# One bank per tile of h, two tiles to a PSUM pair, in an attention and feed-forward kernel

## The chip, the cores and the metric

The kernel runs on one core of one Trainium2 chip. The metric is the device time of one execution in microseconds (us). Matrix products run on TensorE (PE), elementwise work on VectorE (DVE), ScalarE (ACT) and GpSimd (POOL); SyncE (SP) issues DMAs. TensorE writes its results to PSUM, which ACT and DVE read. Each engine works its own list of instructions in order and waits on semaphores that the others raise.

## The reference

For each of 8 batches and 8 heads (576 tokens, head width 64) 32 pack vectors p attend to k and v, the tokens q attend to the packed result, and the outcome goes through a feed-forward layer with g(h) = h cos(h):

```
def sm_attn(qq, kk, vv):
    s = scale * np.matmul(qq, kk.transpose(0, 1, 3, 2))
    s = s - np.max(s, axis=-1, keepdims=True)
    a = np.exp(s)
    a = a / (np.sum(a, axis=-1, keepdims=True) + 1e-09)
    return np.matmul(a, vv)
p_packed = sm_attn(p, k, v)
out = sm_attn(q, p_packed, p_packed)
...
x = out.transpose(0, 2, 1, 3).reshape(4608, 512)
h = x @ w_in            # 512 x 2048
g = h * np.cos(h)
return g @ w_out        # 2048 x 512
```

## The kernel before, in words

**Stages.** A batch b passes through two stretches. In the first the scores are made, exponentials taken, sums and their inverses formed (functions `s1`, `s2`, `sums2`, `normalise`), and the packed values are multiplied into w_in, so that `PPW[b]` (written by `ppw`, four pieces of 512 columns) holds the weights of h for this batch, and `a2n[b]` the normalised second attention. In the second, the **slot** of the batch, h of its 576 tokens is made in 16 tiles of 128 rows, tile number `fc` from 0 to 15. Between tiles stand the output matmuls of the batch before.

**A tile of h before** (`h_mm`): it takes a PSUM pair from `psa()` (two banks of 512 fp32 columns; three pairs in turn in these stretches), splits the 576 tokens into two halves of 288, one to a bank, and makes four matmuls of 288 columns. ACT takes the cosine of both halves in one instruction (`cosT`, as a sine with a bias), and DVE multiplies both with it into `gT[b][:, fc, :]` in one instruction. After tiles 7 and 15 POOL copies tokens 512 to 575 of eight tiles to `joint`, which gathers the last 64 tokens of two batches for one output chunk of 128 tokens.

**Batch 0** is made otherwise: `h_one` makes a tile with tokens 0 to 511 alone, in a single bank, with two matmuls of 512 columns, a cosine and a multiply of 512 columns. Its last 64 tokens of all 16 tiles are made later in one go by `h_rest(0)`, called in slot 1: 32 matmuls of 64 columns into one pair, one cosine and one multiply of 1024 columns, straight into `joint`.

**Output shares.** `out_gen(b)` gives out the output matmuls of batch b one by one, 16 to a chunk of 128 tokens (512 columns each, L351). `fill(n)` puts n of them, called shares here, into TensorE's list. After 16 shares a chunk is copied out of PSUM (`osb`) by ACT in the slots and by DVE between them, and SP sends it to memory. `keep` shares are held back for after the slot.

**The order in a slot** is written out by hand (`slot`): tile fc, its multiply, then its quota of shares, with hooks behind certain tiles. `heavy` gives a tile a greater weight in the quota, and says how many of its shares come behind the hook; `{7: (5, 4)}` is such an entry. The hook after tile 7 (`tiled`) is called the burst here: two pieces of `ppw` for the slot's own batch, then `pp` of the next batch, which writes its result into the unused end of tile 7's pair (`spare`). At the last tile `pp_T` is put ahead of the multiply.

**PSUM and waits.** A pair is given out again when its readers are done. The recording layer works out from the tiles that each instruction reads and writes which others it must wait for, and puts semaphore waits into the lists. Since each engine works in order, whatever stands behind a waiting matmul in TensorE's list waits too.

Of the kernel before, what the change touches and what calls it, by code (L numbers as in the profile page):

```python
# [9 lines left out]
BF16 = mybir.dt.bfloat16  # L10
AF = mybir.ActivationFunctionType
ALU = mybir.AluOpType
PI_HALF = 1.5707963267948966

@with_exitstack
def kernel(
# [10 lines left out]
    nc = tc.nc  # L27
    B, H, S, D = q.shape
# [3 lines left out]
    NFC = DF // 128  # L32
    C = 6
    TP = S // C
    HS = S // 2
# [9 lines left out]
    g_pool = ctx.enter_context(tc.tile_pool(name="g", bufs=2))  # L45
    j_pool = ctx.enter_context(tc.tile_pool(name="joint", bufs=2))
    cos_pool = ctx.enter_context(tc.tile_pool(name="cos", bufs=3))
# [15 lines left out]
    V, ACT, G = nc.vector, nc.scalar, nc.gpsimd  # L63
# [17 lines left out]
    a2u, lns, a2n, PPW = {}, {}, {}, {}  # L81

    def copy(eng, out, in_):
        if eng is ACT:
            ACT.copy(out=out, in_=in_)  # L85
        else:
            eng.tensor_copy(out=out, in_=in_)  # L87

    def psa(dt=FP32):
        return psum["A"].tile([128, 2, 512 if dt == FP32 else 1024], dt, name="psA", tag="A")  # L90
# [5 lines left out]
    def behind(t):  # L96

        G.tensor_copy(out=gate, in_=t)  # L98
# [8 lines left out]
    def pe_T(n, b, engs=(V, V, V), groups=(0, 1, 2), own=None):  # L107
        if 0 in groups:
            xT[n, b] = att_pool.tile([128, H * 3, TP], BF16, name=n + "T", tag=n + "T", bufs=2 if n == "k" else 1)
        t = xT[n, b]  # L110
        flat = bf[n, b].rearrange("p h x -> p (h x)")
        for i in groups:
            ps = own(BF16) if own else psa(BF16)[:, 0, :]
            for j in range(8):
                o = 8 * i + j
                nc.tensor.transpose(ps[:, j * TP:(j + 1) * TP], flat[:, o * 128:(o + 1) * 128],  # L116
                                    ident[0:TP, 0:TP])
            to = t[:, 8 * i:8 * i + 8].rearrange("p a x -> p (a x)"), ps[:, 0:8 * TP]
            if engs[i] is None:
                return to  # L120
            copy(engs[i], *to)
# [72 lines left out]
    def pp_T(b, eng=V, own=None):  # L194
        ps = own(BF16) if own else psa(BF16)[:, 0, :]
        t = pp_sb[b % 2].rearrange("p a d -> p (a d)")
        for i in range(2):
            nc.tensor.transpose(ps[:, i * 128:(i + 1) * 128], t[:, i * D:i * D + 128], ident)
        copy(eng, ppT[b % 2].rearrange("p i x n -> p (i x n)"), ps[:, 0:256])
# [51 lines left out]

    gT, joint = {}, {}

    spare = [None]

    def h_mm(b, fc):
        if fc == 0:
            g_tile(b)
        ps = psa()
        spare[0] = ps[:, 1, HS:512]  # L260
        for y in range(2):
            for e in range(2):
                nc.tensor.matmul(ps[:, e, 0:HS], PPW[b][:, y, fc * 128:(fc + 1) * 128],  # L263
                                 a2n[b][:, y, e * HS:(e + 1) * HS], start=(y == 0), stop=(y == 1))
        cs = cos_pool.tile([128, S], BF16, name="cosT")
        csv = cs.rearrange("p (e x) -> p e x", e=2)
        ACT.activation(out=csv, in_=ps[:, :, 0:HS], func=AF.Sin, bias=PI_HALF)  # L267

        def rest():
            V.tensor_tensor(out=gT[b][:, fc, :].rearrange("p (e x) -> p e x", e=2),  # L270
                            in0=ps[:, :, 0:HS], in1=csv, op=ALU.mult)
            if fc % 8 == 7:
                j0 = (b % 2) * 64
                G.tensor_copy(out=joint[b // 2][:, fc - 7:fc + 1, j0:j0 + 64],  # L274
                              in_=gT[b][:, fc - 7:fc + 1, 512:576])
        return rest

    def g_tile(b):
        gT[b] = g_pool.tile([128, NFC, S], BF16, name="gT", tag="gT")
        if b % 2 == 0:  # L280
            joint[b // 2] = j_pool.tile([128, NFC, 128], BF16, name="joint", tag="joint")

    def h_one(b, fc, own=None):

        if fc == 0:
            g_tile(b)
        ps = (own or one)()
        for y in range(2):
            nc.tensor.matmul(ps, PPW[b][:, y, fc * 128:(fc + 1) * 128], a2n[b][:, y, 0:512],  # L289
                             start=(y == 0), stop=(y == 1))  # L290

        def cos():
            cs = cos_pool.tile([128, 512], BF16, name="cosT")
            ACT.activation(out=cs, in_=ps, func=AF.Sin, bias=PI_HALF)  # L294
            return lambda: V.tensor_tensor(out=gT[b][:, fc, 0:512], in0=ps, in1=cs, op=ALU.mult)  # L295
        return cos

    def h_rest(b):

        t = psa()  # L300
        for fc in range(NFC):
            for y in range(2):
                nc.tensor.matmul(t[:, fc // 8, (fc % 8) * 64:(fc % 8) * 64 + 64],  # L303
                                 PPW[b][:, y, fc * 128:(fc + 1) * 128], a2n[b][:, y, 512:576],
                                 start=(y == 0), stop=(y == 1))
        cs = cos_pool.tile([128, 2, 512], BF16, name="cosR", bufs=1)
        ACT.activation(out=cs, in_=t, func=AF.Sin, bias=PI_HALF)
        j0 = (b % 2) * 64
        V.tensor_tensor(out=joint[b // 2][:, :, j0:j0 + 64],
                        in0=t.rearrange("p a (f x) -> p (a f) x", x=64),  # L310
                        in1=cs.rearrange("p a (f x) -> p (a f) x", x=64), op=ALU.mult)
# [53 lines left out]
    def to_do():  # L365
        return sum(n for _, n in filler)

    def fill(n):
        while n > 0 and filler:
            next(filler[0][0])  # L370
            filler[0][1] -= 1
            if filler[0][1] == 0:
                filler.pop(0)
            n -= 1
# [109 lines left out]
    rest_ppw()  # L484
    fill(7)

    def slot(s, hooks, keep=0, heavy={}, last=None):


        left = to_do() - keep  # L490
        weight = [1 + heavy.get(fc, (0, 0))[0] for fc in range(NFC)]
        for fc in range(NFC):
            rest = h_mm(s, fc)
            if fc == NFC - 1 and last:
                last()
            rest()
            quota = (left * sum(weight[:fc + 1])) // sum(weight) - (left + keep - to_do())
            behind = min(quota, heavy[fc][1]) if fc in heavy else quota
            fill(quota - behind)
            while hooks and hooks[0][0] == fc:  # L500
                hooks.pop(0)[1]()
            fill(behind)

    def pw2(b, n, eng=None):
        ppw(b, n, eng)
        ppw(b, n + 1, eng)

    def tiled(b):


        own, later = spare[0], []
        for n in (2, 3):
            later += ppw(b, n, (ACT, V)[n - 2], later=True)
        later[0]()
        pp(b + 1, V, own=lambda: own)
        later[1]()
# [10 lines left out]
    def cross(n, b):  # L527
        return lambda: xbar(n, b)

    osb_eng[0] = ACT  # L530
    slot(1, [(2, lambda: pw2(1, 2, (ACT, V))), (4, lambda: h_rest(0)), (6, lambda: pack_p(2, 4)), (7, cross("k", 3)),
             (8, tk2), (9, cross("q", 2)), (10, lambda: pe_T("k", 2, (V, V, ACT), (2,)))], 4, {2: (1, 2), 4: (3, 5)})
    ACT.preload_act_table_set(EXP_SET)
    osb_eng[0] = V
    behind(xT["q", 2][0:1, 0, 0:1])
# [33 lines left out]
                                in_=p_bf[:, 8:2 * B].rearrange("p g t d -> p (g t d)"))  # L569
# [2 lines left out]
        load(n, b)  # L572
    fill(9)
    osb_eng[0] = ACT
    slot(2, [(7, lambda: tiled(2))], 10, {7: (5, 4)}, lambda: pp_T(3, V))

    for s in range(3, B):
        nxt = s + 1 < B
        ACT.preload_act_table_set(EXP_SET)
        osb_eng[0] = V  # L580
        set_filler(s - 1)
        fill(5)
        s2(s)
        ppw(s, 0, V)
        fill(8 if nxt else 9)
        if nxt:
            s1(s + 1)
            ppw(s, 1, V)
            a1_xbar(s + 1)
            xbar("q", s + 1)  # L590
            recips(s + 1)
            if s + 2 < B:
                xbar("k", s + 2)
                behind(xT["k", s + 2][0:1, 0, 0:1])
        else:
            for n in range(1, 4):
                ppw(s, n, V)
        fill(4 if nxt else 5)
        sums2(s, 0)
        fill(5)  # L600
        sums2(s, 1)
        normalise(s)
        ACT.preload_act_table_set(SIN_SET)
        fill(13)
        osb_eng[0] = ACT
        for n, b in (("v", s + 2), ("q", s + 2), ("k", s + 3)):
            if b < B:
                load(n, b)
        if nxt:
            slot(s, [(7, lambda: tiled(s))], 5 if s % 2 else 13, {7: (5, 4)}, lambda: pp_T(s + 1, V))  # L610
        else:
            slot(s, [], 5)
    set_filler(B - 1)
    fill(1000)
    tail_chunk(B - 1, 4)
# [30 lines left out]
```

## Time and profile before

| | |
|---|---|
| three runs, us | 245.00, 245.49, 246.91 |
| median | 245.49 |
| the profiled execution's own time | 245.1 |
| its span, first to last instruction | 243.3 |
| mean granted TensorE clock | 0.997 |
| ACT copies of output chunks, mean of one | 583 ns (128x512) |
| POOL copies to `joint` | 14, 8.6 us |
| DMA moved | 37.37 MB, mean 154 GB/s |

How to read the profile's lines. A group line names the kernel's line, engine and operation, what is written and read with partitions x elements, the count, then busy us in all, mean ns of one, and the idle time of the engine just ahead of them with what ended most of it. PEld is TensorE's weight load, which overlaps its matmuls. The chain is followed back from the last instruction: at each step to what released it, or to the instruction before it on its engine. A matmul's end in the profile is modelled and runs past the start of the next one, so its pitch is read from a run of several in the chain, and the idle time of TensorE is counted from that end. PEclk is the granted clock.

### The profile page before, as it was taken

How to read it: one execution, taken by the hardware profiler on the slowest of the kernel's cores; microseconds unless marked ns; L12 is line 12 of the kernel's file. 1: busy time of each engine (PE TensorE's matmuls, PEld its weight loads, DVE VectorE, ACT ScalarE, POOL GpSimd, SP SyncE). 2: the span in 40 equal slices, each digit the busy share in tenths (PEclk: the TensorE clock that was granted, in tenths of full speed). 3: DMA queues.
4: the chain of work that ended last, by engine and by line, in shares of the span. 5: the costliest groups of instructions: out<-in, count | busy, mean ns of one | idle time of the engine just before them, and what ended most of it. 6: DMA issues, size and time to landing. Idle time of an engine off the chain costs nothing.

```text
span 243.3 us, 5484 instructions
## 1 busy us (share of the span) xinstructions
PE 233.8 (96%) x2251; PEld 128.9 (53%) x2251; DVE 162.0 (67%) x256; ACT 166.1 (68%) x267; POOL 37.4 (15%) x60
## 2 busy tenths in 40 slices
PE   7789899999999999999999999999999999999994
PEld 3454354566446564556455654655455645665453
DVE  3259997787568795778758675868667878784001
ACT  2349999778478696868787687858796666773110
POOL 8432230210400041004100510030101010011000
PEclk9999999999999999999999999999999999999998
DMA  6999999999799999997999899999292111311133
GB/s 94 203 205 206 204 206 229 199 237 187 163 184 183 219 179 180 197 197 163 158 199 219 162 221 204 188 164 176 66 192 52 31 46 43 86 36 53 46 84 86
DMA packets 64377, 37.37 MB, mean 154 GB/s; under 512 B 36865, under 2 KB 59777, under 8 KB 64353
## 3 DMA queue, kind: packets, MB, share of 16 engines
q0 software_dynamic: 23152, 18.75, 51.0%
q1 hardware_dynamic: 40960, 18.16, 35.9%
q8 instruction: 17, 0.28, 0.4%
q10 hardware_dynamic: 240, 0.13, 0.2%
q14 instruction: 8, 0.06, 0.1%
HBM read 37.22 MB, written 9.44 MB: 192 GB/s over the span
## 4 chain that ended last, share of the span: by engine, by line
PE 82%; DVE 6%; ACT 1%; issue 1%; ACTq 0%
PE ot L351 50%; PE psA L263 22%; DVE gT L295 3%; PE psA L213 3%; PE psA L143 2%; PE psA L239 2%; PE ot L337 1%; PE psA L186 1%; DVE gT L270 1%; DVE PPW L87 1%; ACT cosT L267 1%; ACT cosT L294 0%; PE psA L116 0%; DVE qT L87 0%; PE psA L303 0%
## 5 line engine op out<-in xcount | busy, mean ns | idle before, releaser
L351 PE MATMUL ot<-w_out_bf,gT 128*128 128x512 bf16 x512 | 134.0, 379 | 0.0
L270 DVE TENSOR_TENSOR gT<-psA,cosT 128x576 bf16<-128x576 f32 x112 | 83.3, 757 | 21.0 <-ACT cosT L267 19.9
L267 ACT ACTIVATE cosT<-psA 128x576 bf16<-128x576 f32 x112 | 72.9, 652 | 24.9 <-PE psA L263 23.5
L263 PE MATMUL psA<-a2n,PPW 128*128 128x288 bf16 x448 | 73.3, 286 | 0.0
L351 PEld LDWEIGHTS <-gT 128*128 128x128 bf16 x512 | 48.2, 98 | 39.5 <-issue 4.2
L263 PEld LDWEIGHTS <-PPW 128*128 128x128 bf16 x448 | 43.8, 98 | 30.1 <-issue 0.4
L87 DVE CAST PPW<-psA 128x1024 bf16<-128x1024 f32 (+1 forms) x24 | 26.8, 1131 | 6.4 <-PE psA L213 6.2
L85 ACT COPY osb<-ot 128x512 f32<-128x512 f32 (+1 forms) x23 | 13.1, 569 | 16.2 <-PE ot L351 13.9
L87 DVE COPY osb<-ot 128x512 f32<-128x512 f32 (+2 forms) x15 | 9.7, 645 | 20.4 <-PE ot L337 17.2
L274 POOL COPY joint<-gT 128x512 bf16<-128x512 bf16 x14 | 8.6, 618 | 78.2 <-DVE gT L270 78.2
L249 DVE SCALAR_TENSOR_TENSOR a2n<-a2u,r,lns 128x576 bf16<-128x576 bf16 x16 | 12.4, 814 | 9.6 <-ACT lns L247 9.6
L152 ACT ACTIVATE a<-psA 128x576 bf16<-128x576 f32 x16 | 10.2, 646 | 8.2 <-PE psA L143 8.2
L241 ACT ACTIVATE lns<-psA 128x576 f32<-128x576 f32 x16 | 10.3, 650 | 7.2 <-PE psA L239 6.7
L351 PE MATMUL ot<-w_out_bf,joint 128*128 128x512 bf16 x48 | 12.2, 380 | 0.0
L98 POOL COPY gate<-kT 1x1 bf16<-1x1 bf16 x4 | 0.7, 180 | 72.7 <-DMA kT<-kbf 72.7
L231 ACT ACTIVATE a2u<-psA,rs 128x576 bf16<-128x576 f32 x16 | 11.0, 737 | 1.1 <-PE psA L143 1.0
L247 ACT ACTIVATE lns<-lns 128x576 f32<-128x576 f32 x16 | 10.0, 673 | 0.0
L213 PE MATMUL psA<-w_in_bf,ppT 64*32 64x512 bf16 x224 | 9.8, 379 | 0.0
L295 DVE TENSOR_TENSOR gT<-psH,cosT 128x512 bf16<-128x512 f32 x15 | 9.3, 680 | 0.4 <-ACT cosT L294 0.4
L391 PE MATMUL ot<-wz 128*128 128x512 f32 (+2 forms) x13 | 7.5, 661 | 1.9 <-DVE wz L404 1.7
L294 ACT ACTIVATE cosT<-psH 128x512 bf16<-128x512 f32 x15 | 8.4, 628 | 0.7 <-DVE gT L295 0.4
L289 PE MATMUL psH<-a2n,PPW 128*128 128x512 bf16 x30 | 7.8, 381 | 0.8 <-DVE PPW L87 0.8
(88 smaller groups left out, 170.6 us busy)
## 6 DMA issues: line engine op xcount, KB each, us to landing
kbf<-in_k_dram POOLq DMA_DIRECT2D x8, 576.0 KB, 14.0
vbf<-in_v_dram POOLq DMA_DIRECT2D x8, 576.0 KB, 7.8
qbf<-in_q_dram POOLq DMA_DIRECT2D x8, 576.0 KB, 10.9
out_dram<-osb SPq DMA_DIRECT2D x24, 192.0 KB, 2.6
out_dram<-osb SPq DMA_DIRECT2D x22, 128.0 KB, 2.9
w_in_bf<-in_moe_w_in_dram POOLq DMA_DIRECT2D x4, 512.0 KB, 17.3
w_out_bf<-in_moe_w_out_dram POOLq DMA_DIRECT2D x4, 512.0 KB, 20.8
out_dram<-osb SPq DMA_DIRECT2D x25, 64.0 KB, 2.3
```

The source lines that it names most:

```text
L85: ACT.copy(out=out, in_=in_)
L87: eng.tensor_copy(out=out, in_=in_)
L152: ACT.activation(out=a1[b % 2][:, y, :, 0:TP].rearrange("p (e m) x -> p e m x", e=2), in_=ps[y][:, :, 0:HS].rearrange("p e (m x) -> p e m ...
L213: nc.tensor.matmul(ps[y][32 * x:32 * x + 32, :], ppT[b % 2][r, 0, x, :], w_in_bf[r, x, n * 512:(n + 1) * 512], start=True, stop=True)
L231: ACT.activation(out=a2u[b][:, y].rearrange("p (e x) -> p e x", e=2), in_=ps[y][:, :, 0:HS], func=AF.Exp, scale=rs1[b][:, y:y + 1])
L241: ACT.activation(out=lns[b][:, y].rearrange("p (e x) -> p e x", e=2), in_=ps[:, :, 0:HS], func=AF.Ln)
L249: V.scalar_tensor_tensor(out=a2n[b][:, y], in0=a2u[b][:, y], scalar=r1[b][:, y:y + 1], in1=lns[b][:, y], op0=ALU.mult, op1=ALU.mult)
L263: nc.tensor.matmul(ps[:, e, 0:HS], PPW[b][:, y, fc * 128:(fc + 1) * 128], a2n[b][:, y, e * HS:(e + 1) * HS], start=(y == 0), stop=(y == 1))
L267: ACT.activation(out=csv, in_=ps[:, :, 0:HS], func=AF.Sin, bias=PI_HALF)
L270: V.tensor_tensor(out=gT[b][:, fc, :].rearrange("p (e x) -> p e x", e=2), in0=ps[:, :, 0:HS], in1=csv, op=ALU.mult)
L295: return lambda: V.tensor_tensor(out=gT[b][:, fc, 0:512], in0=ps, in1=cs, op=ALU.mult)
L351: nc.tensor.matmul(pss[c], w, w_out_bf[:, fc, :], start=(fc == 0), stop=(fc == NFC - 1))
```

## The change

Tiles of h for batches 1 to 7 are now made by `h_one`, as in batch 0: tokens 0 to 511, in one bank, with two matmuls. `half()` gives out the two halves of a pair to two tiles, one after the other; `close_pair()` makes the next tile begin a new pair (at a slot's start, and after tile 0 in slots 2 to 6). `pp` in the burst takes the half behind tile 7. `h_rest` makes the last 64 tokens of a batch after tile 11 (slot 1: after tile 13). `h_mm`, the POOL copies and the 64 last columns of `gT` are gone. In slot 2 the entry for tile 7 goes from (5, 4) to (6, 3).

```
-    def h_mm(b, fc):
...
+    pair = [None, 2]
+    def half():
+        if pair[1] == 2:
+            pair[:] = psa(), 0
+        pair[1] += 1
+        return pair[0][:, pair[1] - 1, :]
+    def close_pair():
+        pair[1] = 2
     def g_tile(b):
-        gT[b] = g_pool.tile([128, NFC, S], BF16, name="gT", tag="gT")
+        gT[b] = g_pool.tile([128, NFC, 512], BF16, name="gT", tag="gT")
...
-    def slot(s, hooks, keep=0, heavy={}, last=None):
+    def slot(s, hooks, keep=0, heavy={}, last=None, alone=()):
+        close_pair()
...
-            rest = h_mm(s, fc)
+            rest = h_one(s, fc, half)()
+            if fc in alone:
+                close_pair()
...
     def tiled(b):
-        own, later = spare[0], []
+        own, later = half(), []
...
-             (8, tk2), (9, cross("q", 2)), (10, lambda: pe_T("k", 2, (V, V, ACT), (2,)))], 4, {2: (1, 2), 4: (3, 5)})
+             (8, tk2), (9, cross("q", 2)), (10, lambda: pe_T("k", 2, (V, V, ACT), (2,))), (13, lambda: h_rest(1))], 4, {2: (1, 2), 4: (3, 5)})
...
-    slot(2, [(7, lambda: tiled(2))], 10, {7: (5, 4)}, lambda: pp_T(3, V))
+    slot(2, [(7, lambda: tiled(2)), (11, lambda: h_rest(2))], 10, {7: (6, 3)}, lambda: pp_T(3, V), (0,))
...
-            slot(s, [(7, lambda: tiled(s))], 5 if s % 2 else 13, {7: (5, 4)}, lambda: pp_T(s + 1, V))
+            slot(s, [(7, lambda: tiled(s)), (11, lambda: h_rest(s))], 5 if s % 2 else 13, {7: (5, 4)},
+                 lambda: pp_T(s + 1, V), (0,))
         else:
-            slot(s, [], 5)
+            slot(s, [(11, lambda: h_rest(s))], 5)
```

The two functions that it calls, which are in the kernel before and stay as they are:

```
    def h_one(b, fc, own=None):
        if fc == 0:
            g_tile(b)
        ps = (own or one)()
        for y in range(2):
            nc.tensor.matmul(ps, PPW[b][:, y, fc * 128:(fc + 1) * 128], a2n[b][:, y, 0:512],
                             start=(y == 0), stop=(y == 1))
        def cos():
            cs = cos_pool.tile([128, 512], BF16, name="cosT")
            ACT.activation(out=cs, in_=ps, func=AF.Sin, bias=PI_HALF)
            return lambda: V.tensor_tensor(out=gT[b][:, fc, 0:512], in0=ps, in1=cs, op=ALU.mult)
        return cos

    def h_rest(b):
        t = psa()
        for fc in range(NFC):
            for y in range(2):
                nc.tensor.matmul(t[:, fc // 8, (fc % 8) * 64:(fc % 8) * 64 + 64],
                                 PPW[b][:, y, fc * 128:(fc + 1) * 128], a2n[b][:, y, 512:576],
                                 start=(y == 0), stop=(y == 1))
        cs = cos_pool.tile([128, 2, 512], BF16, name="cosR", bufs=1)
        ACT.activation(out=cs, in_=t, func=AF.Sin, bias=PI_HALF)
        j0 = (b % 2) * 64
        V.tensor_tensor(out=joint[b // 2][:, :, j0:j0 + 64],
                        in0=t.rearrange("p a (f x) -> p (a f) x", x=64),
                        in1=cs.rearrange("p a (f x) -> p (a f) x", x=64), op=ALU.mult)
```

More of the change, by code (lines that the diff above doesn't have):

```diff
@@ L252 @@
     gT, joint = {}, {}
-    spare = [None]
-    def h_mm(b, fc):
[L257 to L276, printed above, removed]
+    pair = [None, 2]
[6 more added lines that the diff above has]
+        pair[1] = 2
     def g_tile(b):
-        gT[b] = g_pool.tile([128, NFC, S], BF16, name="gT", tag="gT")
+        gT[b] = g_pool.tile([128, NFC, 512], BF16, name="gT", tag="gT")
         if b % 2 == 0:
```

## The prediction

> **What bounds the kernel now.** I read the page's busy shares and chain first, then the chain in order of time inside one slot, then the costliest groups, and last the waits and the timeline around the one place where TensorE waits in a slot. The page:
>
> ```profile
> PE 233.8 (96%) x2251; PEld 128.9 (53%) x2251; DVE 162.0 (67%) x256; ACT 166.1 (68%) x267; POOL 37.4 (15%) x60
> PE 82%; DVE 6%; ACT 1%; issue 1%; ACTq 0%
> ```
>
> TensorE is busy for 96% of the span and carries 82% of the chain that ended last, so the length of its instruction stream, and every gap put into it, is the time. The chain in order of time, in slot 3 and just after it (start, length, what):
>
> ```profile
> 99.85 0.49 PE psA L263 x4
> 100.34 0.22 PE ot L351
> 100.56 0.49 PE psA L263 x4
> 101.05 0.43 PE ot L351 x2
> ...
> 115.92 1.51 PE ot L351 x7
> ```
>
> The work follows without a gap: the four 288-column matmuls of one h tile take 0.49 us, one output share ("f" below) 1.51/7 = 0.216 us. The groups, for the engines behind TensorE:
>
> ```profile
> L270 DVE TENSOR_TENSOR gT<-psA,cosT 128x576 bf16<-128x576 f32 x112 | 83.3, 757 | 21.0 <-ACT cosT L267 19.9
> L267 ACT ACTIVATE cosT<-psA 128x576 bf16<-128x576 f32 x112 | 72.9, 652 | 24.9 <-PE psA L263 23.5
> L295 DVE TENSOR_TENSOR gT<-psH,cosT 128x512 bf16<-128x512 f32 x15 | 9.3, 680 | 0.4 <-ACT cosT L294 0.4
> L294 ACT ACTIVATE cosT<-psH 128x512 bf16<-128x512 f32 x15 | 8.4, 628 | 0.7 <-DVE gT L295 0.4
> ```
>
> ACT and DVE wait for TensorE in the slots, not the reverse. The one wait of TensorE for DVE in a slot is this, in the timeline of slot 2 (start, length, what, idle before):
>
> ```profile
> 80.67 1.42 DVE L270 TENSOR_TENSOR gT<-psA,cosT 128x576 bf16<-128x576 f32 x2 [0.27 <-ACT cosT L267]
> 81.34 0.63 PE L213 MATMUL psA<-w_in_bf,ppT 64*32 64x512 bf16 x16
> 82.15 0.55 PE L186 MATMUL psA<-vbf,a1T 96*32 96x64 bf16 x48 [0.18 <-DVE gT L270]
> ```
>
> pp writes columns 288 to 511 of a bank whose columns 0 to 287 DVE is reading as tile 7 of h, and it starts 0.06 us after that read ends (80.67 + 1.42 = 82.09). Two uses of one PSUM tile, at different columns, are put in order by a wait.
>
> **The change, part by part.** *TensorE's work* stays: before, 16 x 0.49 = 7.84 us per batch. After, 32 matmuls of 512 columns at 0.216 (as L351) are 6.91, and the 32 of 64 columns take 0.93 in the one h_rest of the chain (L303 x32), together 7.84. *DVE* does 16 x 0.680 + 1.225 (the one joint row of before) = 12.1 us per batch instead of 16 x 0.757 = 12.1; *ACT* 16 x 0.628 + 1.023 = 11.1 instead of 10.4; POOL loses 14 copies (8.6 us). These lie beside TensorE and cost nothing in themselves. *The shares in slot 2*: in the built order seven stand ahead of the burst where four stood. The ppw to pp turn took 0.25 us longer there than in the later slots (81.34 to 82.15 is 0.81; from ppw's 107.44 to pp's 108.00 in slot 3's chain it is 0.56), and the three more cover it: a gain of 0.25, and a loss of as much again if that cover is gone.
>
> *What decides is a new wait.* The built program's list of instructions, with the semaphore that each waits for, puts a wait for DVE before the matmuls of every tile that takes the second half of a pair. Counting DVE's updates, the value waited for is the gT multiply of the tile in the first half. So tile 1 of a pair may not start until ACT and DVE are through with tile 0, although the halves are different banks; before, each tile had a pair to itself, and the wait was for a multiply two or three tiles back. TensorE runs in order, so the shares and tiles behind the waiting matmul wait too, and behind them ACT and DVE.
>
> The delay from the first half's start to the second's, from rows: 0.216 to the second matmul, 0.38 until that ends (L289 and L351 rows), 0.04 to ACT (each L267 starts 0.036 after its matmuls), cosT 0.605 (L294: 0.597 at the least, 0.628 mean, behind busy work; 0.652 of L267 less 64 columns at the 0.77 ns by which the 1024 columns of cosR, 1.023, exceed the 512 gives 0.603), 0.03 to DVE, multiply 0.68, and 0.06 back to TensorE: 2.01 us. TensorE has its own 0.432 and the f shares between the halves to fill that. The stall is 2.01 - 0.432 - 0.216 f: 1.36 for f = 1, 1.15 for f = 2, 0.93 for f = 3.
>
> With h_rest after tile 11, DVE multiplies its 1024 columns before tile 12. From tile 11's start: h_rest starts at 0.43, ends at 1.53 (1.10 in the timeline), ACT from 1.57 to 2.59, DVE from 2.62, next DVE work 1.14 later (two DVE casts of this size follow so), tile 12's multiply ends at 4.45, tile 13 may start at 4.51. It would be due at 1.80 + 0.216 x (shares after 11 and 12): stall 2.28 with two shares, 2.06 with three, 1.85 with four.
>
> Shares by slot, from the built order (pairs in slots 2 to 6 are 1-2, 3-4, 5-6, 8-9, 10-11, 12-13, 14-15; tile 7 shares with pp, whose wait lies under the shares and burst between):
> - slot 1 (pairs 0-1 to 14-15): 1.15, then nothing at 2-3 and 4-5, where the PPW burst and the old h_rest cover more than 2.01; 0.93, 0.47 and 0.80 where transposes fill 0.22, 0.68 and 0.35; 1.15; and 1.85 behind h_rest. Sum 6.35.
> - slot 2: four of 1.36, two of 1.15, one 2.28 = 10.02, less the 0.25.
> - slot 3: three of 1.36, three of 1.15, 1.85, and 0.4 where an osb copy on ACT (0.583) stands right ahead of a first half's cosine twice = 9.78.
> - slots 4 and 6: six of 1.15 and 2.06 = 8.96 each; slot 5 with one such osb copy 9.12.
> - slot 7: six of 1.15, 0.93, 1.85, one osb copy = 9.84.
>
> Together 62.8 us in 49 waits. None of it comes back: TensorE has no slack elsewhere for it to be absorbed. 245.1 (the profiled execution; span 243.3 and 1.8 around it) + 62.8 = 307.9, say **308 us**. The profiled execution lies 0.4 below the median of 245.49, which moves nothing here.
>
> Bounds of the chain: with cosT at 0.687, its longest, 2.09, so +4 us; with matmul results taken at the pitch instead of the modelled end (0.17 earlier) 1.84, so -8. I take 2.01, since that modelled end holds in each of the L267 starts to a few ns. An osb copy ahead of every second pair's cosine would add 24 x 0.25 = 6 (the two in slot 3 cost 0.17 and 0.23).
>
> **The rivals.** *The waits are met in time.* They would bite only where less than 2.01 us lies between the halves, that is up to seven shares; the order puts one to three there, and the burst places show it can be covered. If the wait were over by then, the 0.25 would be won, 244.9, and what is late next is tile 15's multiply, whose pair the next scores take: after h_rest DVE runs tiles 12 to 14 back to back at 0.604 (3.70 for six in the chain's L295), a ppT copy 0.24 and tile 15 0.68, so it ends 6.5 us after tile 11's start; TensorE needs the pair there at 6.5 in slots 3 to 6, and at 6.1 in slot 2, with fewer shares. So 244.9 to 245.5, not slower. For it speaks the equal work; against it that the wait stands in the program and pp's 0.18 shows such a wait biting. The Trainium skill, PSUM — Partial Sum Buffer, section "PSUM bank collisions raise a hardware error", asks for a guard by bank and quadrant only: by it the chip would not need this wait, as the halves are two banks, and the sum would be this rival's. No run so far shows the chip without it. Chance 3%.
>
> *The clock falls.* Stalls of 1 to 2 us, 49 times, leave TensorE idle for a third of each slot. At half clock, TensorE's 0.63 in each chain doubles (49 x 0.63 = 31), as do 0.43 and two shares from the second half to the next pair (49 x 0.86 = 42): up to 381 us, 345 if half the slots' time is hit. The windows speak against it (length, PE busy, PEld, DVE, ACT, POOL, PEclk, DMA):
>
> ```profile
> 6.00:9.00 3.00, 1.86 (x20) 0.95 (x20) 0.62 (x2) 0.00 (x0) 2.56 (x4) 1.00 1.29 200
> ```
>
> 1.14 us idle in 3 us, and the granted clock is 1.00. The Trainium skill, TensorE: Matmul & The Clock Gate, section "A second HAM failure mode: psum-queue depth-cycling", says that short idle spells between matmul groups, as PSUM banks are cycled, can make the clock swing between half and full; by it the sum would lie on the way to this rival's. Chance 6%.
>
> *The chain is longer than its rows*, because ACT or DVE is behind by a quarter to a half of a 0.68 multiply at each wait: 49 x 0.17 to 0.34, so 316 to 325. Chance 4%.
>
> **How the numbers follow.** Forecast 87%, with 300 to 318 for the bounds of the chain (-8) and the extra copies (+4 and +6); the three rivals 13%, which the range leaves out but for the start of the last. A measurement tells about 1% from no change. The first rival's 3% lie within 1% of before, but for 1 in 100 that I keep for a gain no row shows. Faster by over 1%: 0.01; within 1%: 0.02; slower: 0.97.
>
> **What would show it.** In the waits of the changed kernel, TensorE's h matmuls waiting for the gT multiply some 49 times, none over 2.3 us, some 55 us in total (63 less 0.165 each, as a matmul's modelled end runs past the next start); PE's busy share down to about 82%; ACT cosT and DVE gT with some 30 and 35 us of the chain, and the seven longest waits behind the joint multiply; PEclk in nines. A PEclk of 5 to 8 in the slots gives the second rival; no such waits gives the first; waits of 1.4 to 1.6 us at two shares the third.

## The result, and the profile after

The changed kernel takes 308.80 us (median of six runs, 308.73 to 308.98), the kernel before 245.38 (six runs); the ratio is 1.2587, interval 1.2565 to 1.2609. The profiled execution took 308.92 us with a span of 307.1, so the span grew by 63.8.

The page of the changed kernel, busy shares, granted clock and chain, and then three of its groups of instructions (busy us, mean ns, idle before and what ended it):

```profile
PE 241.8 (79%) x2251; PEld 112.9 (37%) x2251; DVE 164.2 (53%) x263; ACT 167.7 (55%) x274; POOL 28.9 (9%) x46
...
PEclk9999999999999999999999999999999999999999
...
PE 55%; DVE 20%; ACT 14%; issue 3%; ACTq 0%
...
L283 DVE TENSOR_TENSOR gT<-psA,cosT 128x512 bf16<-128x512 f32 x112 | 77.1, 690 | 71.8 <-ACT cosT L282 71.6
L282 ACT ACTIVATE cosT<-psA 128x512 bf16<-128x512 f32 x112 | 67.0, 598 | 83.6 <-PE psA L277 82.4
L277 PE MATMUL psA<-a2n,PPW 128*128 128x512 bf16 x224 | 66.8, 378 | 56.0 <-DVE gT L283 55.9
```

TensorE, ACT and DVE are busy for about as long as before, within 8 us each, but the span is longer by 64, and the chain now passes through DVE and ACT for a third of it. The group of h's matmuls had no idle time ahead of it before, as its row of that profile shows; now it has 56.0 us, nearly all of it ended by the gT multiply:

```profile
L263 PE MATMUL psA<-a2n,PPW 128*128 128x288 bf16 x448 | 73.3, 286 | 0.0
```

The wait view for TensorE (total us, times, longest) puts that down in one line:

```profile
PE psA L277 <- DVE gT L283: 55.9, 49, 2.1
```

One wait in the timeline, tiles 2 to 4 of slot 3 (start, length, what, idle before):

```profile
118.87 0.59 PE L277 MATMUL psA<-a2n,PPW 128*128 128x512 bf16 x2 [0.98 <-DVE gT L283]
119.30 0.38 PE L339 MATMUL ot<-w_out_bf,gT 128*128 128x512 bf16 x1
119.50 1.30 ACT L282 ACTIVATE cosT<-psA 128x512 bf16<-128x512 f32 x2 [1.41 <-PE psA L277]
119.51 0.59 PE L277 MATMUL psA<-a2n,PPW 128*128 128x512 bf16 x2
119.94 0.59 PE L339 MATMUL ot<-w_out_bf,gT 128*128 128x512 bf16 x2
120.12 1.40 DVE L283 TENSOR_TENSOR gT<-psA,cosT 128x512 bf16<-128x512 f32 x2 [1.31 <-ACT cosT L282]
121.58 0.59 PE L277 MATMUL psA<-a2n,PPW 128*128 128x512 bf16 x2 [1.04 <-DVE gT L283]
```

Tile 3 takes the first half of a pair at 119.51. Tile 4 takes the second half, and starts only at 121.58, 0.06 us after DVE has finished the multiply of tile 3 (120.12 + 1.40 = 121.52). Between them stand two shares, 0.43 us of work. While TensorE waits, ACT and DVE work one after the other, and then they wait for TensorE in turn (1.41 and 1.31 us): the three engines take turns where they overlapped before.

### The profile page after: what moved, and what is told of

Its sections match the earlier page's. It is cut to its first block, busy times and chain, and to the rows that moved or that the text cites. A ratio compares the mean times of both kernels' runs of the same rounds, so it can differ in the third digit from the quotient of the medians.

```text
span 307.1 us, 5465 instructions
## 1 busy us (share of the span) xinstructions
PE 241.8 (79%) x2251; PEld 112.9 (37%) x2251; DVE 164.2 (53%) x263; ACT 167.7 (55%) x274; POOL 28.9 (9%) x46
## 4 chain that ended last, share of the span: by engine, by line
PE 55%; DVE 20%; ACT 14%; issue 3%; ACTq 0%
PE ot L339 30%; PE psA L277 15%; DVE gT L283 15%; ACT cosT L282 9%; DVE joint L297 3%; PE psA L291 2%; ACT cosR L295 2%; PE psA L213 2%; PE psA L143 1%; PE ot L325 1%; DVE PPW L87 1%; PE psA L239 1%; PE psA L186 1%; DVE a2n L249 1%; ACT osb L85 1%
## 5 line engine op out<-in xcount | busy, mean ns | idle before, releaser
L283 DVE TENSOR_TENSOR gT<-psA,cosT 128x512 bf16<-128x512 f32 x112 | 77.1, 690 | 71.8 <-ACT cosT L282 71.6
L282 ACT ACTIVATE cosT<-psA 128x512 bf16<-128x512 f32 x112 | 67.0, 598 | 83.6 <-PE psA L277 82.4
L277 PE MATMUL psA<-a2n,PPW 128*128 128x512 bf16 x224 | 66.8, 378 | 56.0 <-DVE gT L283 55.9
L277 PEld LDWEIGHTS <-PPW 128*128 128x128 bf16 x256 | 24.4, 97 | 95.1 <-issue 70.6
L297 DVE TENSOR_TENSOR joint<-psA,cosR 128x1024 bf16<-128x1024 f32 x8 | 9.8, 1224 | 6.1 <-ACT cosR L295 6.1
L295 ACT ACTIVATE cosR<-psA 128x1024 bf16<-128x1024 f32 x8 | 8.2, 1024 | 3.0 <-PE psA L291 3.0
L291 PEld LDWEIGHTS <-PPW 128*128 128x128 bf16 x256 | 8.5, 98 | 1.9
```

Of the source, the lines that this page charges most:

```text
L297: V.tensor_tensor(out=joint[b // 2][:, :, j0:j0 + 64], in0=t.rearrange("p a (f x) -> p (a f) x", x=64), in1=cs.rearrange("p a (f x) -> p ( ...
```

## The experiments

Two theories stood at the start. **Waits**: the second half of each pair waits for the multiply of the first. **Rival**: the one-bank tiles, with h_rest's long instructions on ACT and DVE, cost the time by themselves. The runs of e1, e2, e3, e6 and e7 were timed against the kernel before, with intervals; the others are one timed execution with its profile, set against the 308.8 of the changed kernel.

**e1: a pair for each tile.** In `slot`:

```
-            if fc in alone:
+            if fc != 7 or s == 1 or s == B - 1:
                 close_pair()
```

> The changed kernel, but every tile of h opens a PSUM pair of its own (tile 7 in slots 2 to 6 excepted, whose second half pp takes), so that no two tiles share one; the 512-column matmuls, h_rest and the shares stay. Waits theory (a second half waits for the multiply of the first half): the 49 waits are gone, in their place the next user of a pair waits for a multiply two or three tiles back, which only bites behind h_rest, where tile 14 takes the pair of the joint multiply, by some 0.6 us a slot: 246 to 251 us. Rival (the cost lies in the one-bank tiles and in h_rest's long instructions on ACT and DVE): 295 us or more, as these are all still there.

Measured 248.67 us, ratio to before 1.0145 (1.0128 to 1.0161). Its waits of TensorE for h:

```profile
PE psA L277 <- DVE joint L297: 2.6, 6, 0.6
```

The 49 waits for the neighbour's multiply are gone, and 60 us with them, though one-bank tiles, h_rest and shares are all there. What is left are six waits for h_rest's multiply, one in each of slots 2 to 7. A wait is longer by starts than in this view, by the 0.16 us that a 512-column matmul's modelled end (0.38) runs past its pitch (0.216): 2.6 + 6 x 0.16 = 3.6, and the run is 3.5 over before. The rival falls.

**e2: six one-bank tiles in the slots.** In `slot`, and likewise in `ppw`, `tiled`, `h_rest` and slot 1's transposes:

```
+        banks(0)
...
-            rest = h_one(s, fc, half)()
+            rest = h_one(s, fc)()
...
+        banks(3)
```

> The changed kernel, but within the slots PSUM is cut into six tiles of one bank instead of three pairs: two neighbouring tiles of h lie in two banks as before, but as tiles of their own; ppw, h_rest, pp, pp_T and slot 1's transposes take single banks too, so ppw and h_rest are read by two instructions of 512 columns instead of one of 1024. Waits theory, with the wait set by the sharing of a tile and not by the chip: TensorE writes one bank while DVE reads the neighbour, without a wait, and the time goes back to 245 to 247 us. If it were the banks themselves that had to wait for each other: 300 us or more.

Measured 246.33 us, ratio 1.0049 (1.0034 to 1.0064). Its waits of TensorE for h, and its timeline at tile 15 of slot 3:

```profile
PE psH L279 <- DVE PPW L87: 2.4, 3, 1.6
```

```profile
116.08 1.34 DVE L285 TENSOR_TENSOR gT<-psH,cosT 128x512 bf16<-128x512 f32 x2
116.09 0.60 ACT L284 ACTIVATE cosT<-psH 128x512 bf16<-128x512 f32 x1
116.33 0.59 PE L279 MATMUL psH<-a2n,PPW 128*128 128x512 bf16 x2
```

TensorE writes tile 15 from 116.33 while DVE and ACT read others out of PSUM, and the view has no h tile that waits for a multiply. Two of the three waits for PPW, 0.8 us, are batch 0's and stood before; the third, 1.6 us, stands at the first change from pairs to banks, in slot 1, and is more than the 1.15 us over before. So the wait belongs to the shared tile, not to the banks.

**e3: the readers of a pair behind both halves' matmuls**, with pairs shared as in the change:

```
-            rest = h_one(s, fc, half)()
+            held.append(h_one(s, fc, half))
...
+            if pair[1] == 2 or fc == 7:
+                rests = [c() for c in held]
```

> The changed kernel with pairs shared as they are, but the cosine and the multiply of both tiles of a pair recorded behind the matmuls of the second. Waits theory: no second half waits any more, since no reader of its pair stands ahead of it; a pair's multiplies end about 2.9 us after its second tile starts, and the next stage's scores need the last pair 2.3 us after, so 0.6 us comes back at five stage ends: 246 to 250 us. Rival (one-bank tiles and h_rest cost it): 295 us or more.

Measured 252.17 us, ratio 1.0281 (1.0266 to 1.0296). The waits:

```profile
PE psA L213 <- DVE gT L283: 3.4, 6, 0.6
...
PE psA L186 <- DVE gT L283: 0.9, 5, 0.2
```

No h matmul waits any longer, so the theory holds, but the time is 2.2 us over the range. I had counted the late multiplies at the stage ends alone, at 0.6 us. They cost 0.72 there (0.55 in the view), at ppw instead of the scores, and once more in slot 1, and in the burst pp waits for tile 7's multiply, some 0.25 us by starts in each of five slots. That makes 5.6 of the 7.0 us over before; the rest is not placed.

**e4 and e5: how the wait depends on what stands between the halves.** In slots 2 to 7 the shares of both tiles of a pair go between its halves (e4), or behind the second (e5):

```
+            upto = fc + 1
+            if s > 1 and pair[1] == 1 and fc != 7:
+                upto = fc + 2        # e5: fc + 0
-            quota = (left * sum(weight[:fc + 1])) // sum(weight) - (left + keep - to_do())
+            quota = (left * sum(weight[:upto])) // sum(weight) - (left + keep - to_do())
```

> The changed kernel, but in slots 2 to 7 the output shares of both tiles of a pair stand between its halves (two to four instead of one or two), and none behind the second. Waits theory: the 49 waits stay, but each gets shorter by 0.216 us for every share moved, 0.43 for two; the next pair then starts right behind the second half and meets the multiply of that half on DVE, which gives back some 0.17: 293 to 301 us, with waits of 0.6 to 0.9 us where 1.04 stood. Rival (a fixed price for each pair or for h_rest, whatever stands between): 308 to 310 us.

> The changed kernel, but in slots 2 to 7 no output share stands between the halves of a pair, all stand behind the second. Waits theory: 79 shares of 0.216 us less cover, so each wait grows to 1.4 to 1.5 us in the wait view and the time by up to 17 us: 323 to 327 us. Rival (a fixed price a pair): 308 to 310 us.

Measured 296.99 and 323.07 us. The waits of e4, then of e5:

```profile
PE psA L277 <- DVE gT L283: 44.2, 49, 1.9
```

```profile
PE psA L277 <- DVE gT L283: 70.6, 49, 1.9
```

The same 49 waits, shorter by 12 and longer by 15 us, as shares move in or out. A fixed price for each pair would have left 308.8 both times. In e5 nothing but the first half's own 0.432 us covers the chain, and its timeline gives the chain bare:

```profile
159.18 0.59 PE L277 MATMUL psA<-a2n,PPW 128*128 128x512 bf16 x2
159.87 0.60 ACT L282 ACTIVATE cosT<-psA 128x512 bf16<-128x512 f32 x1 [0.28 <-PE psA L277]
160.50 0.69 DVE L283 TENSOR_TENSOR gT<-psA,cosT 128x512 bf16<-128x512 f32 x1 [0.66 <-ACT cosT L282]
161.24 0.59 PE L277 MATMUL psA<-a2n,PPW 128*128 128x512 bf16 x2 [1.47 <-DVE gT L283]
```

From 159.18 to 161.24 it is 2.06 us, where I had 2.01.

**e8: h_rest between the halves of pair 12-13**, the hook at 12 instead of 11 (13 in slot 1):

> The changed kernel with h_rest after tile 12 in every slot, between the two halves of pair 12-13, instead of after tile 11 (13 in slot 1). Waits theory: tile 13 waits for tile 12's multiply alone, with h_rest's 0.93 us of matmuls as cover, so 0.1 to 0.5 us instead of 1.8 to 2.3 by starts; tile 15 now waits for tile 14's multiply behind the joint one, 1.34 to 1.55 instead of 1.2 to 1.4. Saved 1.2 to 1.7 us a slot, 10.7 in seven: 297 to 300 us. Rival (h_rest costs the same wherever it stands): 308 to 310 us.

Measured 298.03 us; the waits:

```profile
PE psA L277 <- DVE gT L283: 45.3, 43, 1.4
```

Six of the seven long waits have become so short that the view leaves them out, none is longer than 1.4, and 10.8 us are won by moving h_rest by one tile. The seventh, in slot 2, is still 0.81 us (0.97 by starts, where I gave 0.5 at most): an osb copy on ACT stands ahead of tile 12's cosine there, which starts 0.3 us late. So the long waits were h_rest's multiply ahead of tile 12's on DVE, as the prediction had it.

**e6: the entry (6, 3) alone**, in the kernel before:

```
-    slot(2, [(7, lambda: tiled(2))], 10, {7: (5, 4)}, lambda: pp_T(3, V))
+    slot(2, [(7, lambda: tiled(2))], 10, {7: (6, 3)}, lambda: pp_T(3, V))
```

> The kernel before with the one entry for tile 7 in slot 2 changed from (5, 4) to (6, 3). Prediction's term: pp's wait for tile 7's multiply (0.18 us in the wait view, 0.25 by starts) is gone and 0.1 to 0.3 us is won. Rival (the shares are missing behind the burst, and tile 8 waits for pp's copies instead): 245.2 us, no change, with a new wait at tile 8 of up to 0.3 us.

Measured 245.04 us against 245.08, ratio 0.9999 (0.9990 to 1.0008). The timeline at the burst of slot 2, and at tiles 14 and 15, TensorE first, then ACT and DVE:

```profile
81.50 0.63 PE L213 MATMUL psA<-w_in_bf,ppT 64*32 64x512 bf16 x16
82.06 0.56 PE L186 MATMUL psA<-vbf,a1T 96*32 96x64 bf16 x48
...
87.87 0.65 PE L263 MATMUL psA<-a2n,PPW 128*128 128x288 bf16 x4
88.36 0.38 PE L351 MATMUL ot<-w_out_bf,joint 128*128 128x512 bf16 x1
88.75 0.65 PE L263 MATMUL psA<-a2n,PPW 128*128 128x288 bf16 x4
```

```profile
86.77 0.58 ACT L85 COPY osb<-ot 128x512 f32<-128x512 f32 x1
87.24 1.97 ACT L267 ACTIVATE cosT<-psA 128x576 bf16<-128x576 f32 x3
87.94 2.09 DVE L270 TENSOR_TENSOR gT<-psA,cosT 128x576 bf16<-128x576 f32 x3 [0.27 <-ACT cosT L267]
```

The turn from ppw to pp takes 0.56 us, no longer 0.81, so the cover works. But tile 15 starts 0.39 us after the share ahead of it, whose pitch is 0.216: 0.17 us is lost there, which the kernel before did not lose (88.88 to 89.09). The cause lies on ACT: an osb copy stands ahead of tile 12's cosine, which starts at 87.24, 0.31 us later than its matmuls (86.24 to 86.89) would let it. DVE is idle for 0.27 us until that cosine is done, and ends tile 12's multiply at 87.94 + 0.76 = 88.70. Tile 15, which takes tile 12's pair as the third in turn, starts 0.05 us after that. That it waits for this multiply is read from these times; the view of the chain names no releaser. From its first matmul of h to the next scores, slot 2 lasts 17.09 us here and 17.13 in the kernel before: of the 0.25 next to nothing is left. The rival's place, tile 8, was wrong too.

**e7: the best of e1 and e2**, slot 1 with a pair for each tile, one-bank tiles from slot 2:

```
+            close_pair()
-            rest = h_one(s, fc, half)()
+            rest = h_one(s, fc, one if s > 1 else half)()
+            close_pair()
```

> The changed kernel with six one-bank tiles in slots 2 to 7, as in e2, and in slot 1 a pair for each tile of h, as in e1, which had no wait there, while e2 lost 1.58 us (1.75 by starts) at its first change from pairs to banks. Waits theory: nothing is left of the 49 waits nor of that one, and the 0.25 us at pp in slot 2 is won: 244.3 to 245.0 us, at or a little under the kernel before. Rival (changing from pairs to banks costs at every slot): 246 us as e2.

Measured 245.38 us, ratio 1.0014 (1.0005 to 1.0023): 0.4 us over the range, and no better than the kernel before. One wait in its slots is new, in slot 1, where pack_p takes the pair of the old h_rest:

```profile
PE psA L131 <- DVE joint L301: 0.2, 1, 0.2
```

The other waits of e1 and e2 in the slots are gone. Counted from a slot's first matmul of h to the next scores, slot 2 lasts 16.84 us against 17.13 before, so the gain forecast for it is there. Slot 1 lasts 22.06 against 21.67, and the later slots differ by 0.03 at most. So what is over before lies in slot 1 and ahead of it; that the one wait is all of it isn't shown (slot 1 of e6, the same program as before, differs from before by 0.16).

**e9 and e10: is ACT a link?** One short cosine more ahead of each, in the changed kernel (e9) and in e1 (e10):

```
             cs = cos_pool.tile([128, 512], BF16, name="cosT")
+            if b > 0:
+                ACT.activation(out=cs[:, 0:64], in_=ps[:, 0:64], func=AF.Sin, bias=PI_HALF)
```

> The changed kernel with one more instruction on ACT ahead of each cosine of batches 1 to 7: the cosine of the first 64 columns, made twice. By the rows of 512 and 1024 columns it takes some 0.23 us, of which the next instruction may overlap 0.12. Waits theory: ACT, busy for 55% of the span, is a link of the chain between the halves, so each of the 49 waits grows by 0.11 to 0.23 us: 314 to 320 us. Rival (the waits hang on DVE or on PSUM alone): 308.8 to 310 us.

> The same extra instruction in the kernel of e1, where each tile has a pair of its own. Waits theory: ACT has room there, and only the six waits behind the joint multiply (0.4 to 0.6 us) can feel it: 248.6 to 250 us. Rival (112 more instructions on ACT cost their length anywhere): 258 us or more.

Measured 321.29 and 253.27 us. The waits and the new instruction in e9:

```profile
PE psA L277 <- DVE gT L285: 67.5, 49, 2.4
```

```profile
L283 ACT ACTIVATE cosT<-psA 128x64 bf16<-128x64 f32 x112 | 25.1, 224 | 74.3 <-PE psA L277 74.1
```

The waits grow by 11.6 us, 0.237 each: the whole 0.224 of the new instruction and no overlap, and the time by 12.5, a little above my range. ACT, busy for 55% of the span, is a link of the chain: what is added to it is added to each wait. In e10 the same 25.1 us of ACT cost 4.6 us, more than the 1.3 I allowed and half of the rival's least. Counted from a slot's first matmul of h to the next scores, 3.7 of them lie in slots 1 to 6 and none in slot 7; 0.4 lie ahead of slot 1, where this one execution waited 2.1 us for the first k load and e1's 1.1. Behind each other ACT's two cosines take 0.74 us a tile (their starts at 108.38 and 109.12). Tiles with one share come every 0.65 us, where ACT has no room; those with two, which is the least in slot 7, come every 0.86. So a pair for each tile hides ACT's work only where the tiles leave it the time.

## Why the prediction was right

- **TensorE's work is equal, so only gaps count.** It held: with the gaps out (e7) the new tiles stand within 0.23% of the old ones.
- **Forty-nine waits, one for each second half but those under the bursts.** The view counts 49, with 55.9 us of idle time where I had 55. Taking the sharing away (e1, e2), or the readers out from between the two halves (e3), removed them.
- **The chain.** 2.01 us was predicted, 2.06 measured in e5. The sizes follow: by starts a wait with one share is 1.25 + 0.16 = 1.42 (predicted 1.36), with two 1.04 + 0.16 = 1.20 (1.15), behind h_rest 2.10, 1.89 and 1.67 + 0.16 = 2.26, 2.05 and 1.83 (2.28, 2.06, 1.85). The sum is 55.9 + 49 x 0.16 = 63.7, predicted 63.0, or 62.8 with the 0.25 of slot 2 taken off.
- **What was mis-sized.** ACT's start: 0.036 us after the matmuls was taken; 36 cosines of the changed kernel start some 0.095 after them. The osb copies ahead of a cosine, taken as 0.17 and 0.23, cost 0.055 each (waits of 1.31 beside 1.25 in slot 3). The first adds some 2 us, the second takes off half of one, so the sum is nearer than its parts, in which there is some luck. What such a copy costs depends on when it falls: in e6 and e8 one held a cosine for 0.3.
- **The 0.25 for slot 2's shares** held in the kernel that it was forecast for. There the turn from ppw to pp takes 0.56 us, not 0.81:

```profile
91.89 0.62 PE L213 MATMUL psA<-w_in_bf,ppT 64*32 64x512 bf16 x16
92.45 0.55 PE L186 MATMUL psA<-vbf,a1T 96*32 96x64 bf16 x48
```

Slot 2, from its first matmul of h to the next scores, lasts 27.04 us against 17.13, so 9.91 longer, while its seven waits by starts make 9.13 + 7 x 0.16 = 10.25; in e7, without these waits, it is 0.29 shorter than before. In the kernel before the entry alone wins next to nothing (e6), because TensorE has gained only 0.08 of the 0.25 us when it meets the next limit, tile 12's multiply. The new tiles with the old entry were not run, so how much of the gain is the entry's isn't split off.
- **The signs.** The chain has 29 us of cosT and 45 of gT (14.8% of the span), where I had 30 and 35; some 10 of gT stood in the chain before. TensorE is busy for 79%, not 82%: the 9.5 us that it was idle before the change (243.3 - 233.8) were left out there.
- **The rivals.** The waits were not met in time. Pp's wait, held against that rival, was weaker evidence than it looked: pp writes the very bank that DVE is reading, so it could not tell a wait by tile from a wait by bank; the program's list and e2 do. ACT and DVE were not behind by a quarter of a multiply at each wait. The clock stayed up, though TensorE idled for 31% of slot 4, here in the windows view (length, PE busy, PEld, DVE, ACT, POOL, PEclk, DMA):

```profile
152.00:178.00 26.00, 17.94 (x167) 8.15 (x166) 13.15 (x20) 12.86 (x22) 2.47 (x4) 1.00 0.80 140
```

The Trainium skill's section on psum-queue depth-cycling (TensorE: Matmul & The Clock Gate) let a swing of the clock be feared here; in this kernel stalls of up to 2.3 us, 49 times, did not bring it. The Trainium skill's rule on PSUM (PSUM — Partial Sum Buffer, "PSUM bank collisions raise a hardware error"), by which two banks need no guard against each other, agrees with e2: TensorE wrote one bank while DVE and ACT read others, without a wait. That TensorE wrote the very neighbour bank of one being read, inside one tile, was not tried.

## What to carry to other kernels

Two uses that share a tile may be put in order by the recording layer even where they touch different banks, and the chip then waits: look in the built program for what each wait waits for, before counting a pair as two buffers. Where a wait closes a loop over three engines, price it as the latency of the whole loop less the work that stands between its ends; busy shares of 55% say nothing about it. And a gap on the engine that bounds the kernel is worth what it opens up to the next limit, not its length.

## What was not expected of the hardware

Where ACT had been idle for over 0.1 us, its cosines started 36 ns after the modelled end of their matmuls in the kernel before (all 74) and, but for four, in e1 and e2; in the changed kernel 58 started so, and 36 some 95 ns after. In the program's list both kinds wait for two semaphores, with TensorE's in a different place; that this is the reason was not tried. It adds 0.06 us to the chain at a wait, some 2 us in all.
